# Attention scores from float16 pairs, decay added on GpSimd: one change to a fused attention and feed-forward kernel

## Chip, cores and metric

The kernel runs on one core of a Trainium2 chip. The metric is device time in microseconds (us) of one execution; lower is better. The engines are TensorE (PE; its weight loads are PEld), VectorE (DVE), ScalarE (ACT), GpSimd (POOL) and SyncE (SP), whose queue issues all of this kernel's DMAs in order.

## What is computed

Causal attention with a multiplicative forget gate, then a two-layer feed-forward block, all in float32. There are 8 batches, 8 heads, 576 tokens and 64 columns per head; the feed-forward block goes from 512 to 2048 and back for the 4608 tokens.

```python
scores = scale * np.matmul(q, k.transpose(0, 1, 3, 2))      # scale = 1/8
cum = np.cumsum(np.log(np.clip(f, 0.0001, 1.0)), axis=-1)
decay = cum[:, :, :, None] - cum[:, :, None, :]
scores = np.where(causal, -1000000000.0, scores + decay)
scores = scores - np.max(scores, axis=-1, keepdims=True)
attn = np.exp(scores)
attn = attn / (np.sum(attn, axis=-1, keepdims=True) + 1e-09)
x = np.matmul(attn, v)                                      # heads side by side: 4608 x 512
h = x @ w_in
g = np.where(h >= 1, h, np.where(h <= -1, 0.0, (h + 1) ** 2 / 4))
out = g @ w_out
```

## The kernel before, in words

**Jobs.** The attention is cut into 36 jobs, each a pair of heads of one batch. The first batch is cut in two by rows, so jobs 0 to 3 do its rows 0 to 255 and jobs 4 to 7 the others; from job 8 on each job is a whole pair, four to a batch: batch 1 is jobs 8 to 11, batch 2 jobs 12 to 15. A job goes through blocks of 128 rows (`r` from 0 to 4; the last has 64 rows of both heads stacked on 128 partitions).

**One job.** `load` (L328) brings q and k in two loads and a remainder each, two jobs ahead. `prepare` (L364) turns them with ten TensorE transposes per pair (L374), through PSUM and two ACT copies (L375), into `qkT`: 64 partitions per head, head 0 on partitions 0 to 63 and head 1 on 64 to 127, in float32. `scores` (L409) makes a block's scores by two products into the same PSUM: the float32 product of q and k over 64 rows (L426, `s<-qkT`), and a bfloat16 product over 6 rows (`s<-dec`), whose operands hold 8 times the cumulative log gate in three bfloat16 parts and ones, so that it adds the decay. Those operands are made once by `decay_sums` (L143), written to HBM as `dec_d`, and loaded per job by `load_decay` (L354).

`weights` (L489) takes a block on: a DVE operation (L510) reads the scores from PSUM, adds the causal mask `hide`, scales, keeps the row maximum and writes an SBUF buffer `sdr` (four of them; `sd4`, two, for the last block); ACT does the exponential (L514) and, with the reciprocal sum, the upper float16 half of the weights `pr` (L528), DVE the lower half (L534). A transposing DMA turns them into `pT` (L540, L543), of which there is one buffer, so it waits for the values product of the job before. `values` (L547) is that product (L554): three float16 products, upper by upper, upper by lower and lower by upper, in place of one in float32. Its scale comes from `value_scale` (L255), which loads all of a batch's v through the three buffers `vm` and takes the maximum on DVE (L264). The feed-forward products work on such float16 pairs as well.

**Feed-forward work.** It is done in units of 256 tokens by 256 hidden columns: `moe_front` (L581; 48 or 96 matmuls L596, then ACT, ACT, DVE, ACT, DVE at L605 to L610) and `moe_back` (L617; 12 matmuls L624). Units of finished tokens are spread between the attention blocks; those left over follow the last job.

**Order.** The program is written job by job; a compile-time scheduler then orders each engine's instructions and gives out buffers. An engine runs its list in order. The early jobs, up to about 250 us, run while the weights are loaded and split (`weight_step`), partly on POOL (L242, L243).

Of the kernel before, what the change touches and what calls it, by code (L numbers as in the profile page):

```python
# [16 lines left out]
P = 128  # L17
# [12 lines left out]
NPE = 5  # L30

# [15 lines left out]
def kernel(  # L47
# [93 lines left out]
    dec_d = dram.tile([B * H, NR, 2, S], BF16, name="dec_d")  # L141

    def decay_sums():  # L143
# [5 lines left out]
        rows = rows[0:nb, 0:NR * 2 * S].rearrange("p (r j s) -> p r j s", r=NR, j=2)  # L149
# [11 lines left out]
        rest = fl[0:nb, 0:S]  # L161
        nc.vector.tensor_scalar(out=rest, in0=cum, scalar1=8.0, scalar2=None, op0=ALU.mult)
# [6 lines left out]
        nc.sync.dma_start(dec_d, rows)  # L169


    hide = const.tile([P, FULL], F32, name="hide")
    hide4 = const.tile([P, S], F32, name="hide4")
# [81 lines left out]
    def value_scale(b):  # L255
        m4 = tiny.tile([P, NPAIR], F32, name="m4", bufs=2)
        for i in range(NPAIR):
            if b:
                st = two.tile([P, S], F32, name="vm", bufs=3)
            else:  # L260
                st = stage[:, i * S:(i + 1) * S]
# [11 lines left out]
        scale_of(sv[:, b:b + 1], pv[:, b:b + 1], m)  # L273

# [53 lines left out]
    def load(ji):  # L328
# [3 lines left out]
        w.sps = {}  # L332
# [5 lines left out]
        for j, src in enumerate((q, k)):  # L338
# [5 lines left out]
            dst = x.rearrange("p (t h d) -> p h t d", t=nt, h=2)  # L344
            full = min(w.r1, LAST)
# [8 lines left out]
    def load_decay(w):  # L354
        bh = w.b * H + 2 * w.hp
        w.dec = two.tile([P, 2, S], BF16, name="dec", bufs=3)
        for h in range(2):
            nc.sync.dma_start(w.dec[64 * h:64 * h + NR], dec_d[bh + h])
# [5 lines left out]
    def prepare(w):  # L364

        t_ = two.tile([P, 2, S], F32, name="qkT")
        w.q, w.k = t_[:, 0], t_[:, 1]
# [41 lines left out]
    def scores(w, r):  # L409
# [4 lines left out]
        if r < LAST:  # L414
            outs = [sp[:, h] for h in range(2)]
            w.sps[r] = [sp[:, h, 0:wid] for h in range(2)]
        else:
            flat = sp.rearrange("p h c -> p (h c)")
            outs = [flat[64 * h:64 * h + 64] for h in range(2)]
            w.sps[r] = [flat[:, 0:wid]]  # L420
        for c0 in range(0, wid, 512):
            c1 = min(wid, c0 + 512)
            for x, y, n in ((w.q[:, s0:s1], w.k, D), (w.dec[:, 0, s0 + w.s0:s1 + w.s0], w.dec[:, 1], NR)):
                for h in range(2):
                    rows = slice(64 * h, 64 * h + n)
                    nc.tensor.matmul(  # L426
                        outs[h][:, c0:c1], lhsT=x[rows], rhs=y[rows, c0:c1], start=(n == D), stop=(n == NR)
                    )

# [59 lines left out]
    def weights(w, r):  # L489
# [5 lines left out]
        sds = []  # L495
        for sp in w.sps[r]:
            if r < LAST:
                ring = sdr + more if w.p < NPE else sdr
            else:
                ring = sd4 + [prs[LAST]] if w.p < NPE else sd4  # L500
# [278 lines left out]
```

## Time and profile before

| | |
|---|---|
| median of 3 runs | 1242.38 us (1242.05 to 1242.46) |
| profiled execution: time | 1243.96 us |
| profiled execution: span of the core | 1242.1 us |
| mean granted TensorE clock | 0.959 |
| PE busy | 1151.3 us, 93% of the span |
| DVE busy | 736.0 us, 59% |
| ACT busy | 763.9 us, 62% |
| POOL busy | 46.4 us, 4% |
| DMA queue that moves the data | 42.7% of 16 engines' span |

The profile is one execution with every instruction's start and end. A row of a grouped view reads: line, engine, operation, output and inputs by the program's names, shape, count, then busy time, mean ns of one, and the idle time of the engine just before. Matmuls are pipelined, so the duration of one holds the time through the array too; what a run of matmuls costs is read from the start of its first to the start of what follows.

### The profile page before, as it was taken

The page shows a single profiled execution, that of the slowest core. Times are in us where ns is not written, and L with a number is a line of the kernel's source. Part 1 is how long each engine was busy: PE and PEld are TensorE (multiplying, and loading weights), DVE is VectorE, ACT ScalarE, POOL GpSimd, SP SyncE. Part 2 cuts the span into 40 slices and gives each one's busy share as a digit, 9 for nine tenths or more (in the row PEclk, how much of TensorE's full clock was granted, in tenths as well). Part 3 has the DMA queues.
Part 4 walks back from the last instruction along what each step waited for, and adds up shares of the span by engine and source line. Part 5 has one row for each costly group of instructions (what it writes and reads, how often), then busy time and mean ns, then how long its engine had stood idle before and what let it go on. Part 6 is the DMA issues. An engine that isn't in the chain of part 4 may idle for free.

```text
span 1242.1 us, 23800 instructions
## 1 busy us (share of the span) xinstructions
PE 1151.3 (93%) x9124; PEld 713.1 (57%) x9124; DVE 736.0 (59%) x2063; ACT 763.9 (62%) x1565; POOL 46.4 (4%) x56
## 2 busy tenths in 40 slices
PE   1778677799899999999999999999999999999998
PEld 0544334455466666666666665655666566577665
DVE  6869877777755755565555555566556655522222
ACT  3666545686766666666566556666766666643443
POOL 2021332000000000000000000000000000000000
PEclk9969767799899999999999999999999999999999
DMA  8854454555854444545414433444643443220000
GB/s 259 278 135 102 140 149 112 106 113 119 166 102 101 93 100 83 101 83 101 69 43 73 100 66 77 81 88 86 115 87 82 85 90 68 50 48 2 18 17 17
DMA packets 336817, 118.21 MB, mean 95 GB/s; under 512 B 321296, under 2 KB 321296, under 8 KB 336640
## 3 DMA queue, kind: packets, MB, share of 16 engines
q1 hardware_dynamic: 336704, 116.70, 42.7%
q8 instruction: 71, 1.16, 0.4%
q14 instruction: 42, 0.34, 0.1%
HBM read 56.72 MB, written 10.32 MB: 54 GB/s over the span
## 4 chain that ended last, share of the span: by engine, by line
PE 79%; ACT 1%; DVE 1%; SPq 0%; DMA 0%; issue 0%; ACTq 0%
PE ph L596 30%; PE po L624 29%; PE s L426 8%; PE big L554 5%; PE big L426 4%; PE big L374 3%; ACT pr L528 0%; DVE sdr L510 0%; DMA qk<-in_q_dram 0%; PE s L132 0%; SPq L543 0%; ACT vs L397 0%; DVE ot L637 0%; SPq L390 0%; DVE pr L534 0%
## 5 line engine op out<-in xcount | busy, mean ns | idle before, releaser
L596 PE MATMUL ph<-x,place 128*128 128x256 f16 (+3 forms) x4608 | 436.6, 250 | 6.7 <-ACT x L563 2.9
L624 PE MATMUL po<-place,g 128*128 128x512 f16 x1728 | 411.3, 380 | 3.8 <-ACT g L609 3.7
L596 PEld LDWEIGHTS <-place 128*128 128x128 f16 x4608 | 356.5, 99 | 71.5 <-issue 9.8
L624 PEld LDWEIGHTS <-g 128*128 128x128 f16 x1728 | 163.0, 98 | 172.7 <-issue 6.6
L514 ACT ACTIVATE sdr<-sdr,nm 128x384 f32<-128x384 f32 (+1 forms) x248 | 137.5, 556 | 106.9 <-DVE nm L510 105.3
L607 DVE SCALAR_TENSOR_TENSOR u<-ph,z,u 128x512 f32<-128x512 f32 x136 | 101.8, 749 | 148.1 <-ACT u L606 147.0
L605 ACT ACTIVATE u<-ph,z 128x512 f32<-128x512 f32 x136 | 104.7, 770 | 106.3 <-PE ph L596 105.8
L534 DVE SCALAR_TENSOR_TENSOR pr<-sdr,rc,pr 128x384 f16<-128x384 f32 (+2 forms) x232 | 120.6, 554 | 60.2 <-ACT pr L528 60.2
L609 ACT ACTIVATE g<-u,z 128x512 f16<-128x512 f32 x136 | 97.9, 720 | 93.8 <-DVE u L607 93.8
L610 DVE SCALAR_TENSOR_TENSOR g<-u,z,g 128x512 f16<-128x512 f32 x136 | 102.0, 750 | 78.8 <-ACT g L609 78.7
L528 ACT ACTIVATE pr<-sdr,rc 128x384 f16<-128x384 f32 (+1 forms) x236 | 120.5, 557 | 23.4 <-ACT sdr L514 16.8
L426 PE MATMUL s<-qkT 64*128 64x128 f32 (+3 forms) x512 | 115.9, 504 | 15.0 <-DVE nm L510 11.1
L510 DVE CUSTOM_DVE_ANT_0 sdr<-s,hide 128x384 f32<-128x384 f32 (+1 forms) x248 | 112.3, 490 | 27.0 <-PE s L426 26.9
L606 ACT ACTIVATE u<-u 128x512 f32<-128x512 f32 x144 | 89.8, 624 | 2.6
L374 PE MATMUL big<-ident,qk 128*128 128x128 f32 (+1 forms) x328 | 62.9, 302 | 19.5 <-DMA qk<-in_q_dram 4.5
L522 DVE TENSOR_SCALAR rc<-sm 128x2 f32<-128x2 f32 (+1 forms) x149 | 24.5, 165 | 93.9 <-ACT sdr L514 86.4
L426 PEld LDWEIGHTS <-dec 6*128 6x128 bf16 (+1 forms) x384 | 19.3, 95 | 103.1 <-issue 80.2
L554 PE MATMUL big<-pT,vs 128*64 128x320 f16 (+3 forms) x1098 | 73.3, 284 | 0.5 <-DVE nm L510 0.4
L374 PEld LDWEIGHTS big<-ident,qk 128*128 128x128 f32 (+1 forms) x328 | 42.9, 153 | 45.6 <-issue 23.2
L426 PEld LDWEIGHTS s<-qkT 64*128 64x128 f32 x512 | 44.4, 197 | 42.4 <-DVE nm L510 14.6
L554 PEld LDWEIGHTS <-vs 128*64 128x64 f16 x1098 | 50.2, 112 | 27.9 <-issue 9.7
L375 ACT ACTIVATE qkT<-big 128x576 f32<-128x576 f32 (+2 forms) x72 | 43.4, 603 | 26.1 <-PE big L374 25.8
(142 smaller groups left out, 857.8 us busy)
## 6 DMA issues: line engine op xcount, KB each, us to landing
out_dram<-ot SPq DMA_DIRECT2D x36, 256.0 KB
qk<-in_k_dram SPq DMA_DIRECT2D x64, 128.0 KB
vm<-in_v_dram SPq DMA_DIRECT2D x28, 288.0 KB
v<-in_v_dram SPq DMA_DIRECT2D x62, 128.0 KB
qk<-in_q_dram SPq DMA_DIRECT2D x56, 128.0 KB
place<-in_moe_w_in_dram SPq DMA_DIRECT2D x12, 512.0 KB
place<-in_moe_w_out_dram SPq DMA_DIRECT2D x10, 512.0 KB
x<-in_moe_w_out_dram SPq DMA_DIRECT2D x6, 512.0 KB
```

The source lines that it names most:

```text
L374: nc.tensor.transpose(pt[:, c0:c0 + m], w.x32[j][0:m, c0:c0 + P], ident[0:m, 0:m])
L426: nc.tensor.matmul(outs[h][:, c0:c1], lhsT=x[rows], rhs=y[rows, c0:c1], start=(n == D), stop=(n == NR))
L510: nc.vector.tensor_tensor_reduce(out=a, in0=sp, in1=hide[:, FULL - wid:FULL] if r < LAST else hide4, scale=-0.125, scalar=BIG, op0=ALU.add ...
L514: nc.scalar.activation(a, a, AF.Exp, bias=nm[:, i:i + 1], scale=-1.0, accum_out=sm[:, i:i + 1])
L528: nc.scalar.activation(pr[:, :, 0, i, :], a, AF.Copy, scale=rc[:, i:i + 1])
L534: nc.vector.scalar_tensor_tensor(out=pr[:, :, 1, i, :], in0=a, scalar=rc[:, i:i + 1], in1=pr[:, :, 0, i, :], op0=ALU.mult, op1=ALU.subtract,)
L554: nc.tensor.matmul(av[64 * h:64 * h + 64, at + s0:at + s1], lhsT=w.vs[:, vl, h, t, :], rhs=w.pT[:, t, pl, h, s0:s1], start=(t == 0 and pi ...
L596: nc.tensor.matmul(ph[:, fi, a0:a1], lhsT=wi[fb][:, wl, t, fi * P:(fi + 1) * P], rhs=xs[b][:, t, xl, s0:s0 + a1 - a0], start=(fi == 0 and ...
L605: nc.scalar.activation(u, h, AF.Relu, scale=z.u[:, i:i + 1], bias=z.h[:, i:i + 1])
L607: nc.vector.scalar_tensor_tensor(out=u, in0=h, scalar=z.t[:, i:i + 1], in1=u, op0=ALU.max, op1=ALU.min)
L610: nc.vector.scalar_tensor_tensor(out=g[:, 1], in0=u, scalar=z.r[:, i:i + 1], in1=g[:, 0], op0=ALU.mult, op1=ALU.subtract)
L624: nc.tensor.matmul(po[ch][i], lhsT=g[:, gl, fi * TC + i * P:fi * TC + (i + 1) * P], rhs=wo[fb][:, wl, fi, :], start=(first and fi == 0 and ...
```

## The change

It has three parts.

1. **Decay on POOL from job 8 on.** The cumulative log gates go to HBM in float32 (`cum_d`), and `load_decay` loads one row per head, broadcast to 128 partitions, into a ring of three buffers `ck`. Per block and head, POOL writes the decay of that block into the `sdr` or `sd4` buffer with a `tensor_scalar` (row gate minus column gate, times a scale) and masks the diagonal square with `affine_select`. DVE's operation then takes that buffer where it took `hide`. The 6-row product is left to jobs 0 to 7, and `dec_d` holds 8 heads in place of 64. The column values come from five more TensorE transposes at the start.
2. **q and k in float16 pairs from job 12 on.** `query_scale` loads all of a batch's q and k once more, eight loads through the `ck` ring, with one DVE maximum each, and makes scales by batch. `prepare` then makes the upper halves on ACT and the lower ones on DVE, in one buffer `qs`, and turns them with one transposing DMA into `qkT`. The scores are three float16 products over 64 rows.
3. **Buffers.** `value_scale` uses the `ck` ring, too; the mask `hide` lies in `qs` for the early jobs.

```diff
+NQK = 12
+NDEC = 8
...
     def load_decay(w, h):
+        bh = w.b * H + 2 * w.hp + h
+        if w.p >= NDEC:
+            ck = two.tile([P, S], F32, name="ck", bufs=3)
+            nc.sync.dma_start(ck, cum_d[bh:bh + 1].broadcast_to([P, S]))
...
+    def query_scale(b):
+        ms = tiny.tile([P, 2, NPAIR], F32, name="m8", bufs=2)
+        for j, src in enumerate((q, k)):
+            for i in range(NPAIR):
+                st = two.tile([P, S], F32, name="ck", bufs=3)
...
+                nc.sync.dma_start(st, part)
+                nc.vector.tensor_reduce(
+                    out=ms[:, j, i:i + 1], in_=st, axis=AX.X, op=ALU.max, apply_absolute_value=True
+                )
...
     def prepare(w):
+        t_ = two.tile([P, 2, 2, SP], F16, name="qkT")
+        if w.p >= NQK:
...
+            w.qk = [(t_[:, 0, lq], t_[:, 1, lk]) for lq, lk in ((0, 0), (0, 1), (1, 0))]
+            qs = one.tile([P, 2, 2, SP], F16, name="qs")
+            for j in range(2):
+                sc = sqk[:, j, w.b:w.b + 1]
+                nc.scalar.activation(qs[:, j, 0], w.x32[j], AF.Copy, scale=sc)
+                nc.vector.scalar_tensor_tensor(
+                    out=qs[:, j, 1], in0=w.x32[j], scalar=sc, in1=qs[:, j, 0], op0=ALU.mult, op1=ALU.subtract
+                )
+            nc.sync.dma_start_transpose(
...
     def scores(w, r):
+        terms = [(x[:, s0:s1], y, D) for x, y in w.qk]
+        if w.p < NDEC:
+            terms.append((w.dec[:, 0, s0 + w.s0:s1 + w.s0], w.dec[:, 1], NR))
...
+        for h in range(2):
+            p0, p1 = (0, P) if r < LAST else (64 * h, 64 * h + 64)
+            sd = sds[h % len(sds)][0]
+            nc.gpsimd.tensor_scalar(
+                out=sd[p0:p1, 0:wid], in0=w.ck[h][p0:p1, 0:wid], scalar1=w.nsig if w.p < NQK else w.nsig[p0:p1],
+                scalar2=w.cqs[p0:p1, r, h:h + 1], op0=ALU.mult, op1=ALU.add,
+            )
+            nc.gpsimd.affine_select(
...
```

The order of instructions shows it at two places. The first is PE at a job's first block: `s` is the scores' PSUM, `qkT` the turned q and k, `ph` and `place` a feed-forward product. Before:

```order
L374 MATMUL big<-ident,qk_1_127 128x64
L426 MATMUL s<-qkT 128x128 x2
L426 LDWEIGHTS dec
L426 MATMUL s<-dec 128x128
L426 LDWEIGHTS dec
L426 MATMUL s<-dec 128x128
```

And with the change:

```order
L511 LDWEIGHTS qkT
L511 MATMUL s<-qkT 128x128
L511 LDWEIGHTS qkT
L511 MATMUL s<-qkT 128x128
L511 LDWEIGHTS qkT
L511 MATMUL s<-qkT 128x128
L511 LDWEIGHTS qkT
L511 MATMUL s<-qkT 128x128
L690 LDWEIGHTS place_107
L690 MATMUL ph<-x,place_107 128x256
```

The transposes are gone from PE there, and the float32 product and the 6-row product of two heads have become three float16 products of two heads (the first two of the six lie ahead of these rows), most of them with nothing in between.

The second place is SP, in the later part of the program. Before, between the transposing transfers of two jobs, stand the loads of v, of the next q and k, and of the decay:

```order
L543 DMA_TRANSPOSE pT<-pr_5646 128x10x64 x2
L390 DMA v_128<-in_v_dram 128x4x64 x2
L392 DMA v_128<-in_v_dram 64x2x64
L347 DMA qk_0_126<-in_q_dram 128x4x64 x2
L351 DMA qk_0_126<-in_q_dram 64x2x64
L347 DMA qk_0_126<-in_k_dram 128x4x64 x2
L351 DMA qk_0_126<-in_k_dram 64x2x64
L644 DMA out_dram<-ot 128x512 x2
L358 DMA dec<-dec_d 6x1152 x2
L540 DMA_TRANSPOSE pT<-pr_5761 128x4x128
```

With the change, where `query_scale` falls, in the second job of each batch (`ck` is the ring of three, `cum_d` the gates):

```order
L306 DMA ck<-in_q_dram 128x576
L400 DMA qk_1_133<-in_k_dram 128x4x64
L404 DMA qk_1_133<-in_k_dram 64x2x64
L306 DMA ck<-in_q_dram 128x576
L306 DMA ck<-in_k_dram 128x576 x4
L411 DMA ck<-cum_d 128x576 x2
L436 DMA_TRANSPOSE qkT<-qs 128x20x128
L634 DMA_TRANSPOSE pT<-pr_5342 128x4x128
L634 DMA_TRANSPOSE pT<-pr_5372 128x8x128
```

The loads of the ring, and the transfer that turns q and k, have moved in ahead of the transposing transfers of the weights. DVE's list has the matching eight maxima there, between feed-forward operations.

123 lines of the change are left out of this document (90 added, 33 removed).

## The prediction, as it was put on record

> **What bounds the kernel now.** I read the page first for the busiest engine, then a table by stage, then the stage that is longest. The page gives TensorE:
>
> ```profile
> PE 1151.3 (93%) x9124; PEld 713.1 (57%) x9124; DVE 736.0 (59%) x2063; ACT 763.9 (62%) x1565; POOL 46.4 (4%) x56
> ```
>
> A share of 93% is a mean, so I cut the span in four. The columns are the stretch, its length, then busy time and count of PE, PEld, DVE, ACT and POOL, granted clock, DMA share and GB/s; the last row counts the values product alone.
>
> ```profile
> 0.00:250.00 250.00, 167.72 (x905) 97.69 (x906) 192.35 (x601) 139.12 (x310) 46.44 (x56) 0.82 0.58 160
> 250.00:340.00 90.00, 85.75 (x645) 48.72 (x643) 64.36 (x206) 66.42 (x150) 0.00 (x0) 0.94 0.65 132
> 340.00:1086.00 746.00, 745.98 (x6337) 462.92 (x6333) 435.71 (x1200) 493.14 (x1013) 0.00 (x0) 1.00 0.43 84
> 1086.00:1242.00 156.00, 151.86 (x1246) 103.81 (x1245) 43.58 (x58) 65.24 (x94) 0.00 (x0) 1.00 0.08 22
> ```
> ```profile
> 340.00:1086.00 746.00, 53.24 (x828) 35.81 (x828) 1.00 0.43 84
> ```
>
> From 340 to 1086 us PE has no idle time at full clock, and the other engines have room. The values product has 36 matmuls in a job, so its 828 are 23 jobs: a job takes 746 / 23 = 32.4 us, in which DVE works 18.9, ACT 21.4, and the DMA engines 0.43 x 32.4 = 13.9. What leaves PE here leaves the time, until something else is late. Before 250 us PE is one third idle; the last stretch is feed-forward work, which the change leaves alone.
>
> **What the change takes from PE.** One job on PE in order of time (start, length, then the group; I read from start to start):
>
> ```profile
> 604.99 2.25 PE L554 MATMUL big<-pT,vs 128*64 128x64 f16 x36
> 607.17 2.85 PE L596 MATMUL ph<-x,place 128*128 128x192 f16 x48
> 609.86 2.75 PE L624 MATMUL po<-place,g 128*128 128x512 f16 x12
> ...
> 617.72 0.80 PE L374 MATMUL big<-ident,qk 128*128 128x128 f32 x5
> 618.26 0.54 PE L426 MATMUL s<-qkT 64*128 64x128 f32 x4
> 618.73 0.23 PE L426 MATMUL s<-dec 6*128 6x128 bf16 x2
> 618.89 1.48 PE L596 MATMUL ph<-x,place 128*128 128x192 f16 x23
> 620.21 0.80 PE L374 MATMUL big<-ident,qk 128*128 128x128 f32 x5
> 620.95 0.43 PE L596 MATMUL ph<-x,place 128*128 128x64 f16 x5
> 621.30 0.70 PE L426 MATMUL s<-qkT 64*128 64x256 f32 x4
> 621.94 0.28 PE L426 MATMUL s<-dec 6*128 6x256 bf16 x2
> 622.15 1.29 PE L596 MATMUL ph<-x,place 128*128 128x192 f16 x20
> ...
> 626.30 0.92 PE L426 MATMUL s<-qkT 64*128 64x384 f32 x4
> 627.14 0.33 PE L426 MATMUL s<-dec 6*128 6x384 bf16 x2
> 627.41 2.52 PE L596 MATMUL ph<-x,place 128*128 128x192 f16 x42
> ...
> 632.45 1.13 PE L426 MATMUL s<-qkT 64*128 64x512 f32 x4
> 633.51 0.39 PE L426 MATMUL s<-dec 6*128 6x512 bf16 x2
> 633.83 2.79 PE L596 MATMUL ph<-x,place 128*128 128x256 f16 x24
> ...
> 639.14 1.08 PE L426 MATMUL big<-qkT 64*64 64x512 f32 x4
> 640.15 0.40 PE L426 MATMUL big<-dec 6*64 6x512 bf16 x2
> 640.48 0.33 PE L426 MATMUL big<-qkT 64*64 64x64 f32 x4
> 640.75 0.21 PE L426 MATMUL big<-dec 6*64 6x64 bf16 x2
> 640.89 0.28 PE L596 MATMUL ph<-x,place 128*128 128x256 f16 x1
> ```
>
> The transposes take 0.54 + 0.74 = 1.28 us. The five score blocks take 0.63 + 0.85 + 1.11 + 1.38 + 1.75 = 5.72, of which the decay products are 0.16 + 0.21 + 0.27 + 0.32 + 0.47 = 1.43.
>
> In their place from job 12 on stand three float16 products over 128 + 256 + 384 + 512 + 576 = 1856 columns, both heads side by side. The trace has no such product over 64 rows, so I bound it. The nearest row is L554: float16, two heads side by side, weights of its own for each matmul; it passes 3 x 1600 columns in 2.18 us, 0.454 ns per column with the weight loads in it. So 3 x 1856 columns take 2.53 us. Leaving the 64-row form costs something: the first decay product takes 0.16 for 128 columns worth 0.06, so 0.10 per block; the order has about five groups a job, so 0.5. That makes 3.03, and I take it. The low end is L596, 24 x 256 columns in 2.69, 0.438 ns, with no cost of leaving: 2.44. The high end prices every product like a decay product: 3 x 1.43 = 4.29.
>
> The Trainium skill ("TensorE: Matmul & The Clock Gate", Part 3 on row and column tiling) says that a weight load overlaps matmuls in flight only when it goes to another row group. By it the next product of the same head could not load early, and the price would be near the high end; the L554 row, all 128 rows and the same row groups, disagrees, but it is tiled by columns. It stands below as a rival.
>
> So a job saves 5.72 - 3.03 + 1.28 = 3.97 us, and 24 jobs 95.3. Jobs 8 to 11 lose the decay product alone: 4 x 1.43 = 5.7. Six scales of q and k add two small PE steps each, which I put at 0.5, like the five transposes' 0.54: 3.0. The balance is 98.0; between the ends it is 24 x 2.71 + 5.7 - 3 = 68 and 24 x 4.56 + 5.7 = 115.
>
> **What it adds elsewhere.** The rows for it are groups by shape (busy us, mean ns, idle before), ACT, DVE and POOL in turn:
>
> ```profile
> L375 ACT ACTIVATE qkT<-big 128x576 f32<-128x576 f32 x60 | 38.7, 646 | 22.4 <-PE big L374 22.1
> L397 ACT ACTIVATE vs<-v,sv 128x640 f16<-128x640 f32 x31 | 25.6, 826 | 24.0 <-PE big L554 16.4 <-DVE sv L112 4.3 <-DVE gm L104 2.2
> ```
> ```profile
> L398 DVE SCALAR_TENSOR_TENSOR vs<-v,sv,vs 128x640 f16<-128x640 f32 x31 | 27.3, 882 | 15.6 <-ACT vs L397 15.5
> L264 DVE TENSOR_REDUCE m<-vm 128x1 f32<-128x576 f32 x28 | 20.3, 743 | 10.6 <-DMA vm<-in_v_dram 10.5
> L245 DVE SCALAR_TENSOR_TENSOR place<-place,sw,place 128x512 f16<-128x512 f32 x10 | 7.4, 744 | 1.4 <-ACT place L240 1.4
> L245 DVE SCALAR_TENSOR_TENSOR place<-x,sw,place 128x512 f16<-128x512 f32 x6 | 5.1, 861 | 0.7 <-ACT place L240 0.7
> ```
> ```profile
> L242 POOL TENSOR_SCALAR place<-place,sw 128x512 f32<-128x512 f32 x12 | 9.7, 821 | 106.9 <-ACT place L240 106.9
> ```
>
> With the saving a job would take 32.4 - 4.0 = 28.4 us. ACT trades two copies of 0.646 for two of 0.826: 21.8 us, 77%. DVE gains two lower halves at 0.882, eight maxima per four jobs at 0.743, and as many as four more that the shared ring moves here from the early stage: 18.9 + 1.76 + 1.49 + 0.74 = 22.9, 81%. POOL writes 3712 columns a job at 0.821 / 512 us, which is 6.0, and ten masks that I put at 0.3 (128 columns at that rate are 0.21): 9 us. None is full, so I cost them at nothing while their inputs come in time. If that cover goes, the scores' PSUM is not read, and PE stops at the next score block.
>
> SP's rows (start, time of the issues) for one job before:
>
> ```profile
> 607.27 6.76 SPq L540 DMA_TRANSPOSE pT<-pr  x4
> 614.12 2.96 SPq L543 DMA_TRANSPOSE pT<-pr  x2
> ...
> 639.80 0.94 SPq L644 DMA_DIRECT2D out_dram<-ot  x2
> ```
>
> SP has the weights' transfers out at 617, then issues q, k and v, and is at its next output at 639.80. The new transfer is moved ahead of them: it has 20 squares where those four have 40, so about 3.4 us of issue, for 24 jobs. The transposed weights of that job are used from 644 on, so 3.4 us are hidden by more than 20. On the DMA engines a job adds 0.66 MB of transposing, 0.59 of gates and 0.59 of q and k; at the stage's 84 GB/s for 0.43 of the engines that is 9.4 us, 13.9 to 23.3, or 82%.
>
> The ring is the new wait. While `query_scale` loads, two of its three buffers are free at most, so eight loads go in four rounds, each waiting for a maximum in DVE's list, and behind the loads on SP stand the gates, the turned q and k and the transposed weights. The nearest row is L264: 10.5 us of waiting in 28 maxima, 0.375 each. The 48 new ones then wait 18 us on DVE; I take half of it, 9, as reaching PE, between nothing and the rival below. At the start the smaller `dec_d`, the added gates and five transposes on an idle PE I take at nothing, as also the moved maxima.
>
> The sum: 98 - 9 = 89. The profiled execution took 1243.96, its span 1242.1 and the rest outside; 1243.96 - 89 = 1155, and the median lies 1.6 lower: 1153 us.
>
> **Rivals.** First, exposed weight loads over 64 rows: the high price, 24 x 1.26 = 30 us less gain, 1183. The L554 row speaks against it. Chance 0.12.
>
> Second, loads become late. In the stretch from 250 to 340, with jobs as short as the new ones, PE idled 4.25 us of 90 at a DMA share of 0.65, and the chain of waits has there
>
> ```profile
> 322.18 2.25 DMA qk<-in_q_dram
> ```
>
> That rate, 4.7% of the 648 us that the long stage would have left, is 31 us, for my 9: 1175. If the ring stops PE, a round is 0.6 of issue, 2.25 of load and 0.743 of maximum, four rounds 14.4; half of that in six batches is 43: 1187. Chance 0.20.
>
> Third, it ends slower: POOL holds up DVE. The Trainium skill ("GPSIMD Engine Reference", 1. Specifications) says that the two share their SBUF interfaces, with contention when DVE reads two SBUF inputs, as L534 and L610 do. If DVE stood for all of POOL's 9 us, and 1.5 us a load for three loads a job (four times L264's mean), a job would cost DVE 22.9 + 9 + 4.5 = 36.4, for PE's old 32.4: 24 x 4.0 = 96 slower, 1338. It decides from the point where 5 of POOL's 9 us stop DVE. For it speaks L245, 744 ns in one form and 861 in the other while POOL worked nearby; but 16% of 9 us is 1.4. Chance 0.08.
>
> Fourth, it does not do what it says: the heads' products run one after the other. That doubles 2.53 us: 61 less gain, 1214. The last block's decay product, two heads with 512 columns in 0.33 us where one after the other needs 0.45, speaks against. Chance 0.05.
>
> **How the numbers follow.** The forecast has 0.55: from 1127 (a saving of 115, nothing given back) to some 1170. The range must leave out 2 in 10 at most; from 1128 the first two rivals bring it to 1195, and the other two, 0.13, stay out with the tails. A measurement of this kernel can tell about 0.2% from no change. Faster has the forecast and rivals one, two and four less a little for unclear ends, 0.90; rival three splits into 0.08 slower and, with the rest, 0.02 the same.
>
> **What would show it.** Right: no transposes from job 12 on; score blocks of about 0.27, 0.45, 0.62, 0.80 and 0.88 us from start to start; PE still full from 340 us on, with jobs of about 28 us. Wrong: blocks at three times the decay product; PE idle before score blocks, ended by DVE's L604, with DVE waiting for `ck` loads or POOL; DVE operations with two SBUF inputs longer than now by much more than 16%; or a DMA share near 1.

## The result, and the profile after

| | before | after |
|---|---|---|
| median | 1242.22 us (1241.60 to 1242.46, 4 runs) | 1289.21 us (1283.95 to 1293.72, 4 runs) |
| span of the profiled execution | 1242.1 us | 1285.8 us |
| PE busy | 1151.3 us | 1081.4 us |
| PE idle (span less busy) | 90.8 us | 204.4 us |

The kernel became slower: the ratio is 1.0378, with a 95% interval of 1.0336 to 1.0419. The forecast was 1153 us, 136 less than what came. The last two lines of the table already hold the story: PE works 69.9 us less and idles 113.6 us more, and 113.6 - 69.9 is the 43.7 us by which the span grew. The engines' row of the page after:

```profile
PE 1081.4 (84%) x8859; PEld 688.2 (54%) x8859; DVE 837.0 (65%) x2227; ACT 763.1 (59%) x1564; POOL 373.6 (29%) x620
```

No engine is full any more. So the question goes from "who is busiest" to "what is waited for, and where". The table by stage, with the columns of the prediction's table, and one worse stretch of 50 us below it:

```profile
0.00:250.00 250.00, 172.42 (x932) 101.45 (x933) 187.20 (x585) 139.43 (x310) 68.98 (x102) 0.81 0.55 145
250.00:340.00 90.00, 60.48 (x427) 35.33 (x426) 54.92 (x144) 46.75 (x100) 27.12 (x50) 0.82 0.71 148
340.00:1086.00 746.00, 653.21 (x5861) 420.20 (x5861) 525.04 (x1379) 481.71 (x1003) 270.80 (x455) 0.94 0.70 144
...
300.00:350.00 50.00, 18.07 (x113) 9.73 (x114) 30.56 (x101) 21.69 (x52) 20.43 (x37) 0.58 0.92 187
```

and the same 50 us of the kernel before:

```profile
300.00:350.00 50.00, 45.73 (x400) 27.50 (x398) 37.15 (x125) 36.38 (x81) 0.00 (x0) 0.90 0.66 142
```

In the first 250 us little changed (932 matmuls for 905). From 250 us on PE stands: 29.5 us of 90 (4.3 before), then 92.8 of 746 (none before). The granted clock goes with it, 0.94 in place of 1.00 in the long stage, and 0.58 where PE idles most. There the matmuls themselves are slower, too: the four float32 ones over 512 columns in the first row below take 2.08 us, where the same four took 1.13 in the prediction's rows. The Trainium skill ("TensorE: Matmul & The Clock Gate", Part 1) says that the clock is held down by default and released by a busy PE; these rows agree.

The worst stretch shows one turn of the mechanism. PE first (start, length, group, and in brackets the idle time before and who ended it):

```profile
313.81 2.08 PE L511 MATMUL s<-qkT 64*128 64x512 f32 x4 [3.15 <-DVE nm L604]
323.66 4.26 PE L648 MATMUL big<-pT,vs 128*64 128x64 f16 x36 [7.78 <-DVE nm L604]
328.67 0.39 PE L690 MATMUL ph<-x,place 128*128 128x192 f16 x4 [0.74 <-ACT x L657]
330.71 0.93 PE L511 MATMUL big<-qkT 64*64 64x512 f16 x12 [1.66 <-DVE x L658]
331.57 1.03 PE L690 MATMUL ph<-x,place 128*128 128x192 f16 x8
337.96 0.37 PE L125 MATMUL s<-ident,m 128*1 128x128 f32 x1 [5.36 <-DVE m L287]
```

DVE at the same time:

```profile
315.75 1.15 DVE L628 SCALAR_TENSOR_TENSOR pr<-sdr,rc,pr 128x384 f16<-128x384 f32 x2 [0.73 <-ACT pr L622]
320.96 0.75 DVE L283 TENSOR_REDUCE m<-ck 128x1 f32<-128x576 f32 x1 [4.07 <-DMA ck<-in_v_dram]
321.63 0.68 DVE L604 CUSTOM_DVE_ANT_0 sdr<-s,sdr 128x512 f32<-128x512 f32 x1
...
322.85 0.75 DVE L604 CUSTOM_DVE_ANT_0 sd<-big,sd 128x576 f32<-128x576 f32 x1
...
336.96 0.75 DVE L283 TENSOR_REDUCE m<-ck 128x1 f32<-128x576 f32 x1 [5.09 <-DMA ck<-in_v_dram]
```

And SP's queue:

```profile
305.70 6.59 SPq L634 DMA_TRANSPOSE pT<-pr  x4
312.39 3.15 SPq L637 DMA_TRANSPOSE pT<-pr  x2
315.65 0.53 SPq L411 DMA_DIRECT2D ck<-cum_d  x1
316.28 0.38 SPq L282 DMA_DIRECT2D ck<-in_v_dram  x1
...
324.09 0.52 SPq L282 DMA_DIRECT2D ck<-in_v_dram  x1
...
328.19 0.34 SPq L282 DMA_DIRECT2D ck<-in_v_dram  x1
328.64 4.54 SPq L634 DMA_TRANSPOSE pT<-pr  x3
333.29 0.96 SPq L282 DMA_DIRECT2D ck<-in_v_dram  x1
```

POOL reads the gates in `ck`; the row with `nsig` is of job 12, the one with `cq` of job 11:

```profile
305.81 0.82 POOL L521 TENSOR_SCALAR sd<-ck,nsig,cqs 64x576 f32<-64x576 f32 x1
...
312.62 1.53 POOL L521 TENSOR_SCALAR sdr<-ck,cq 128x512 f32<-128x512 f32 x2
```

At 316 the scores of 512 columns lie ready in PSUM, and the DVE operation that takes them (L604) has its decay written. But ahead of it in DVE's list stands a maximum of v (L283), whose load was issued at 316.28 only, behind six transposing transfers in SP's order. Until 314.15 all three buffers held gates: two those of job 11, which POOL still read, and the third one of job 12, in use since 305.81. DVE stands 4.07 us, then takes the scores of this block and, at 322.85, those of the last one, whose PSUM (`big`) the values product needs; by then PE has idled 7.78. The other three loads of that batch's v follow one by one, at 324, 328 and 333, between other transfers, and the last makes DVE stand 5.09 us and PE 5.36. In the grouped rows this is the idle time before the maxima:

```profile
L307 DVE TENSOR_REDUCE m<-ck 128x1 f32<-128x576 f32 x48 | 36.1, 752 | 42.4 <-DMA ck<-in_q_dram 21.9 <-DMA ck<-in_k_dram 20.5
L283 DVE TENSOR_REDUCE m<-ck 128x1 f32<-128x576 f32 x28 | 21.0, 751 | 32.2 <-DMA ck<-in_v_dram 32.1
```

42.4 + 32.2 = 74.6 us of DVE standing at maxima, where the kernel before had 10.6.

What the change does to PE came as forecast. Score blocks of one or another job, each with the group behind it:

```profile
739.68 0.34 PE L511 MATMUL s<-qkT 64*128 64x128 f16 x6
739.96 0.39 PE L690 MATMUL ph<-x,place 128*128 128x256 f16 x2
...
743.86 0.50 PE L511 MATMUL s<-qkT 64*128 64x256 f16 x6
744.29 1.59 PE L690 MATMUL ph<-x,place 128*128 128x256 f16 x13
...
748.84 0.66 PE L511 MATMUL s<-qkT 64*128 64x384 f16 x6
749.43 2.36 PE L690 MATMUL ph<-x,place 128*128 128x256 f16 x20
...
754.75 0.82 PE L511 MATMUL s<-qkT 64*128 64x512 f16 x6
755.50 2.36 PE L690 MATMUL ph<-x,place 128*128 128x256 f16 x20
...
789.14 0.93 PE L511 MATMUL big<-qkT 64*64 64x512 f16 x12
790.00 0.28 PE L690 MATMUL ph<-x,place 128*128 128x256 f16 x1
```

From start to start 0.28, 0.43, 0.59, 0.75 and 0.86 us, in sum 2.91, for a forecast of 0.27, 0.45, 0.62, 0.80 and 0.88.

### The profile page after: what moved, and what is told of

The parts are those of the page before. It is cut to its first block, busy times and chain, and to the rows that moved or that the text cites. A ratio compares the mean times of both kernels' runs of the same rounds, so it can differ in the third digit from the quotient of the medians.

```text
span 1285.8 us, 24565 instructions
## 1 busy us (share of the span) xinstructions
PE 1081.4 (84%) x8859; PEld 688.2 (54%) x8859; DVE 837.0 (65%) x2227; ACT 763.1 (59%) x1564; POOL 373.6 (29%) x620
## 3 DMA queue, kind: packets, MB, share of 16 engines
q8 instruction: 69, 1.13, 0.4%
## 5 line engine op out<-in xcount | busy, mean ns | idle before, releaser
L690 PE MATMUL ph<-x,place 128*128 128x256 f16 (+3 forms) x4608 | 450.8, 253 | 44.0 <-ACT x L657 25.6
L690 PEld LDWEIGHTS <-place 128*128 128x128 f16 x4608 | 368.8, 101 | 133.2 <-issue 59.7
L521 POOL TENSOR_SCALAR sdr<-ck,nsig,cqs 128x128 f32<-128x128 f32 (+1 forms) x192 | 160.7, 841 | 270.9 <-DVE pr L628 264.6
L628 DVE SCALAR_TENSOR_TENSOR pr<-sdr,rc,pr 128x384 f16<-128x384 f32 (+2 forms) x232 | 125.5, 574 | 34.5 <-ACT pr L622 34.2
L511 PE MATMUL s<-qkT 64*128 64x128 f16 (+5 forms) x704 | 92.3, 363 | 45.1 <-DVE nm L604 40.0
L604 DVE CUSTOM_DVE_ANT_0 sdr<-s,sdr,nalpha 128x128 f32<-128x128 f32 (+1 forms) x192 | 99.6, 546 | 34.3 <-POOL sdr L525 17.3
L521 POOL TENSOR_SCALAR sd<-ck,nsig,cqs 64x576 f32<-64x576 f32 x48 | 44.4, 926 | 233.4 <-DMA ck<-cum_d 162.6
L525 POOL TENSOR_SCALAR_AFFINE_SELECT sdr<-sdr 128x128 f32<-128x128 f32 x224 | 78.1, 360 | 8.4
L511 PEld LDWEIGHTS <-qkT 64*128 64x128 f16 (+1 forms) x864 | 34.7, 100 | 72.8 <-issue 54.3
L307 DVE TENSOR_REDUCE m<-ck 128x1 f32<-128x576 f32 x48 | 36.1, 752 | 42.4 <-DMA ck<-in_q_dram 21.9
L433 DVE SCALAR_TENSOR_TENSOR qs<-qk,sqk,qs 128x640 f16<-128x640 f32 x48 | 42.0, 906 | 17.6 <-ACT qs L432 17.6
```

Source lines behind the costliest of these rows:

```text
L511: nc.tensor.matmul(outs[h][:, c0:c1], lhsT=x[rows], rhs=y[rows, c0:c1], start=(i == 0), stop=(i == len(terms) - 1),)
L521: nc.gpsimd.tensor_scalar(out=sd[p0:p1, 0:wid], in0=w.ck[h][p0:p1, 0:wid], scalar1=w.nsig if w.p < NQK else w.nsig[p0:p1], scalar2=w.cqs[p ...
L604: nc.vector.tensor_tensor_reduce(out=a, in0=sp, in1=other, scale=w.nalpha, scalar=BIG, op0=ALU.add, op1=ALU.min, accum_out=nm[:, i:i + 1],)
L628: nc.vector.scalar_tensor_tensor(out=pr[:, :, 1, i, :], in0=a, scalar=rc[:, i:i + 1], in1=pr[:, :, 0, i, :], op0=ALU.mult, op1=ALU.subtract,)
L690: nc.tensor.matmul(ph[:, fi, a0:a1], lhsT=wi[fb][:, wl, t, fi * P:(fi + 1) * P], rhs=xs[b][:, t, xl, s0:s0 + a1 - a0], start=(fi == 0 and ...
```

## The experiments

Theory 1: the `ck` ring, shared by the gates and the maxima of q, k and v, makes the maxima's loads late, and DVE stands at them. Theory 2: POOL and DVE hold each other up where both access SBUF. Theory 3: the way through the four score buffers has become longer, since POOL must write one before DVE can use it. All runs at a glance; "DVE at maxima" is DVE's idle time before the maxima of q, k and v, summed (L283 and L307 after the change):

| run | median us | 95% interval of the ratio to before | DVE at maxima, us |
|---|---|---|---|
| before | 1242.2 | | 10.6 |
| after | 1289.2 | 1.0336 to 1.0419 | 74.6 |
| two rings of two (rings22) | 1208.5 | 0.9704 to 0.9735 | 21.5 |
| fixed scale (fixed_scale) | 1211.7 | 0.9713 to 0.9765 | 42.3 |
| decay alone (decay_alone) | 1227.0 | 0.9834 to 0.9902 | 30.7 |
| POOL twice (pool_twice) | 1348.9 | 1.0823 to 1.0867 | 73.3 |
| ring of four, shared (ck4) | 1245.3 | 1.0003 to 1.0033 | 64.9 |
| loads spread (spread) | 1270.6 | 1.0180 to 1.0258 | 77.5 |
| two rings, fixed scale (rings22_fixed) | 1179.7 | 0.9462 to 0.9509 | 11.8 |
| pairs alone (pairs_alone) | 1247.4 | 1.0029 to 1.0056 | 33.2 |
| gates from POOL's queue (gates_poolq) | 1290.4 | 1.0334 to 1.0434 | 60.8 |
| two rings, POOL twice (rings22_pool2) | 1221.7 | 0.9791 to 0.9833 | 30.8 |
| two rings, loads held (rings22_hold) | 1221.2 | 0.9795 to 0.9863 | 45.9 |
| the same, gates from POOL's queue (rings22_hold_poolq) | 1235.0 | 0.9914 to 0.9944 | 49.6 |
| three and one (rings31) | 1240.5 | 0.9974 to 1.0004 | 66.4 |
| three and one, fixed scale (rings31_fixed) | 1182.5 | 0.9481 to 0.9551 | 25.1 |
| three and two (rings32) | 1221.3 | 0.9816 to 0.9864 | 33.4 |
| two and three (rings23) | 1207.3 | 0.9693 to 0.9742 | 21.5 |
| a scale by pair (pair_scale) | 1232.0 | 0.9898 to 0.9946 | 82.8 |
| two rings, constants for the scale (rings22_loads) | 1211.4 | 0.9742 to 0.9790 | 34.4 |

The last column alone doesn't give the time: with the loads spread DVE stands 3 us longer than after the change and the kernel is 19 us faster; with the gates from POOL's queue it stands 14 us less and nothing is gained. What stands behind a maximum in DVE's list counts as well.

### Is it the ring, the maxima, or POOL?

**Two rings of two.**

```diff
 def value_scale(b), def query_scale(b):
-                st = two.tile([P, S], F32, name="ck", bufs=3)
+                st = two.tile([P, S], F32, name="vm", bufs=2)
 def load_decay(w, h):
-            ck = two.tile([P, S], F32, name="ck", bufs=3)
+            ck = two.tile([P, S], F32, name="ck", bufs=2)
```

> Two buffers for the gates and two of their own for the maxima of q, k and v, in place of three shared. Theory 1 (the shared ring: the two gates hold two of three buffers until POOL's last write of a job, the maxima's loads go through the third one at a time, and SP, in order, keeps the turned q and k and the turned weights behind them; DVE stands at the maxima): the loads no longer wait for gates, so most of the 122 us of idle TensorE between 250 and 1120 us goes: 1180 to 1230 us. Theory 2 (POOL and DVE hold each other up) and theory 3 (the longer way through the four score buffers, which POOL must write before DVE and gets back only from DVE's lower half): the same as changed, 1275 to 1295.

1208.5 us: 81 us come back, and the kernel is 2.8% faster than the one before. The same loads, the same maxima, the same work on POOL. DVE's rows for the maxima:

```profile
L307 DVE TENSOR_REDUCE m<-vm 128x1 f32<-128x576 f32 x48 | 35.5, 746 | 11.7 <-DMA vm<-in_k_dram 8.0 <-DMA vm<-in_q_dram 3.5
L283 DVE TENSOR_REDUCE m<-vm 128x1 f32<-128x576 f32 x28 | 20.6, 746 | 9.8 <-DMA vm<-in_v_dram 9.8
```

They stand 53 us less, and the time fell by more than that. DVE's operation L604 also waits less for POOL's mask, 6.7 us for 22.4, and at a higher clock (0.931 for 0.915 in the mean) the same 8859 matmuls keep PE busy for 1067.7 us in place of 1081.4. The loads of q and k, issued between 244 and 935 us in the changed kernel, are all issued by 406 us here. It isn't the amount of DMA traffic: in the long stage its share is 0.68 for 0.70, and yet PE idles 31 us there in place of 93:

```profile
340.00:1086.00 746.00, 714.76 (x6571) 455.86 (x6572) 526.54 (x1399) 523.20 (x1081) 275.40 (x469) 0.97 0.68 132
```

Theory 1 holds for the larger part.

**A fixed scale** in place of `query_scale`'s loads, maxima and small steps.

```diff
 def query_scale(b):
-        for j, src in enumerate((q, k)):
...
-        across(mk, m2)
-        sc = sqk[:, :, b]
-        scale_of(sc, mk, mk)
...
+        nc.vector.memset(sqk[:, :, b], 256.0)
+        nc.vector.memset(nsig[:, b:b + 1], -8.0 * 65536.0)
+        nc.vector.memset(nalpha[:, b:b + 1], -0.125 / 65536.0)
```

> q and k are scaled by 256 in every batch: the 48 loads of q and k for the maxima, their 48 maxima and the two small TensorE steps a batch are left out; the maxima of v stay in the shared ring. Theory 1: two thirds of what goes through the ring beside the gates is gone, and with it most of the idle TensorE: 1170 to 1220 us. Theories 2 and 3: POOL's work and the score buffers are as they were; only 48 x 0.74 = 36 us of DVE's 837 go, which is not full: 1265 to 1290.

1211.7 us: 78 us, as theory 1 has it. What is left in the shared ring, the maxima of v, still makes DVE stand 42.3 us.

**The decay alone**, with q and k in float32 to the end.

```diff
-NQK = 12
+NQK = 36
```

> The decay on POOL from batch 1 on, q and k in float32 with transposes on TensorE to the end, as before the change. It leaves out the pairs: no maxima of q and k, no turned q and k by transfer. TensorE loses 28 decay products of 1.43 us, 40 us. Theory 1: the maxima of v still meet the gates in the ring, seven times, which gives back some 10 to 25 us: 1210 to 1235. Theory 2 or 3: POOL's 28 jobs cost what they cost in the changed kernel, and the time is above the one before: 1250 to 1290.

1227.0 us: theory 1's range. POOL and the gates by themselves gain 15 us on the kernel before, though PE works 38 us less (1113.2 for 1151.3).

**POOL's writes twice.**

```diff
+            for _ in range(2):
                 nc.gpsimd.tensor_scalar(
...
                 )
```

> Each of POOL's writes of the decay is made twice, with the same result: POOL works 6 us more a job, 28 jobs. Theory 1: POOL is in use 29% of the time, the second write is late only where DVE waits for POOL now (22 us of DVE's waits in all): 1290 to 1320. Theory 2 (the port): the cost of POOL's work beside DVE doubles: if it is what makes the 140 us between forecast and result, 1370 or more. Theory 3 (the way through the score buffers): 1.6 us more for each 512-column write in a chain of five a job, 3 to 5 us a job: 1370 to 1430.

1348.9 us, 60 more than the changed kernel: above what theory 1 said and below the others. So POOL's time did count, and the next question was by which way. The same two lines of doubling on top of the two rings:

> Two rings of two (1208.5) with each of POOL's writes made twice. In the shared ring that cost 1349 - 1289 = 60 us. If POOL's time is paid by itself, through the score buffers or the port: again 50 to 60, 1260 to 1270. If it is paid through the ring, since the gates' buffers are held until POOL's last write of a job and the maxima wait for them: at most a third of it, 1210 to 1230.

1221.7 us, 13 more than two rings alone, where the shared ring paid 60. So POOL's work is paid mostly through the ring. Not by longer standing at the maxima, though: that is 73.3 us with the doubled writes and 74.6 without. What grew is DVE's wait for POOL's mask, from 22.4 to 58.9 us in the shared ring, and from 6.7 to 14.5 in two rings. A likely reason is that its gates come late in the shared ring: with the doubled writes POOL waits 158 us for them there, and 87 in two rings.

**The pairs alone**, decay on TensorE to the end, maxima in a ring of two.

```diff
-NDEC = 8
+NDEC = 36
...
-    NDH = NDEC // (2 * NPAIR) * H
+    NDH = B * H
...
+    hide = const.tile([P, FULL], BF16, name="hide")
+    hide4 = const.tile([P, S], BF16, name="hide4")
...
-                st = two.tile([P, S], F32, name="ck", bufs=3)
+                st = two.tile([P, S], F32, name="vm", bufs=2)
```

> The pairs as in the changed kernel with the maxima in a ring of two of their own, the decay on TensorE in every batch, so no gates and no POOL; its decay rows are not scaled, so that part of what is computed is left out, and the mask is a constant in bfloat16 in place of float32. It gives back 28 decay products of 1.43 us, 40 us, beside the run with two rings (1208.5): 1248 if POOL and gates cost nothing there; with 55 us lost to POOL's way through the score buffers and to the gates, 1190 to 1200; between these in proportion.

1247.4 us, the 1248 of the case in which POOL and gates cost nothing once the rings are apart. In sum, that is: in the first 250 us PE idles 9 us more than with two rings (99.5 for 90.1), and from there on 12 less (38.0 for 50.1). So theories 2 and 3 can have a share of some 12 us once the rings are apart, as the 13 us for the doubled writes also suggest, but not the bulk.

### What in the ring: the order on SP, the number of buffers, or the eight in a row?

**A ring of four, shared**, at all three places:

```diff
-                st = two.tile([P, S], F32, name="ck", bufs=3)
+                st = two.tile([P, S], F32, name="ck", bufs=4)
```

> One ring of four buffers for gates and maxima, where two rings of two gave 1208.5. If it is the number of buffers that counts: 1200 to 1220. If it is that the maxima stand in the same queue for buffers as the gates, which are held until POOL's last write of a job: the ring gains one buffer for four rounds of loads, two at a time now, and some half of the 80 us come back: 1235 to 1265.

1245.3 us, 44 of the 81: the case in which sharing counts, not only the number. DVE still stands 64.9 us.

**Loads spread**: `query_scale` made a generator that yields behind each maximum, one taken per step.

```diff
             nc.sync.dma_start(st, part)
             nc.vector.tensor_reduce(
                 out=ms[:, j, i:i + 1], in_=st, axis=AX.X, op=ALU.max, apply_absolute_value=True
             )
+            yield
...
+                    scans.append(query_scale(w.b + 1))
+                for _ in range(1 if scans else 0):
+                    if next(scans[0], 0) == 0:
+                        scans.pop()
```

> The ring of three as in the changed kernel, the same loads and maxima, but the eight loads of q and k are written one to a step over two jobs (nine steps) in place of eight at once in one step. Theory 1: a load waits alone for the third buffer and SP and DVE don't stand for eight in a row; the part that q and k have in the loss (78 us by the run with a fixed scale) goes but for the loads themselves: 1210 to 1240. If it is the total of work and loads, or POOL's way through the score buffers, nothing changes: 1275 to 1295.

1270.6 us, a miss: 19 us in place of 50 to 80. It isn't that eight loads stand in a row. One by one they wait as long, 77.5 us in all.

**Gates from POOL's queue.**

```diff
-            nc.sync.dma_start(ck, cum_d[bh:bh + 1].broadcast_to([P, S]))
+            nc.gpsimd.dma_start(ck, cum_d[bh:bh + 1].broadcast_to([P, S]))
```

> The shared ring of three as in the changed kernel, but the gates' loads are issued from POOL's queue in place of SP's. If what costs is that SP stands before a gate's load until a buffer is free, with the turned q, k and weights behind it: 1210 to 1240. If it is the ring itself (the loads for the maxima wait for buffers whose gates are in use, and DVE's list stands at the maxima, whoever issues): 1270 to 1300. POOL then also issues 56 loads, at no price that a run has shown yet.

1290.4 us, no change. I had also held SP's order to be guilty, since the gates stand in it ahead of the turned q, k and weights. Taking them out of it gives nothing in sum: after 250 us PE idles 19 us less (108.1 for 126.8), and in the first 250 us 12 more (90.1 for 77.6). So a part of the loss, up to these 19 us, may lie in SP's order; the rest is not in it.

**On which side of the parted ring a buffer counts.** Three for the gates and one for the maxima:

```diff
-                st = two.tile([P, S], F32, name="ck", bufs=3)
+                st = two.tile([P, S], F32, name="vm", bufs=1)
...
             ck = two.tile([P, S], F32, name="ck", bufs=3)
```

> Three buffers for the gates, one for the maxima (four in all, as with two and two, 1208.5). If the gates hold things up (POOL waited 130 us for their loads with two buffers): 1185 to 1200. If the maxima do, with one buffer each load waits for the maximum before it: 1220 to 1245.

1240.5 us, with four buffers as in two and two. Its rows for the maxima:

```profile
L307 DVE TENSOR_REDUCE m<-vm 128x1 f32<-128x576 f32 x48 | 36.0, 749 | 46.4 <-DMA vm<-in_q_dram 23.4 <-DMA vm<-in_k_dram 22.8
L283 DVE TENSOR_REDUCE m<-vm 128x1 f32<-128x576 f32 x28 | 20.9, 747 | 20.0 <-DMA vm<-in_v_dram 20.0
```

With one buffer, each load starts only when the maximum before it is done, and DVE stands nearly as in the shared ring of four (66.4 for 64.9). So it is the maxima that want the buffers, not the gates. In the shared ring of three the gates of the running job hold two buffers, and the maxima live on the third, when the next job's first gate doesn't hold it. Three and two, and two and three, with the room from the decay rows of the first batch:

```diff
-            w.dec = two.tile([P, 2, S], BF16, name="dec")
+            w.dec = two.tile([P, 2, S], BF16, name="dec", bufs=1)
```

> Three buffers for the gates and two for the maxima; the room comes from the decay rows of batch 0, which have one buffer in place of two (up to 2 us in each of 7 early jobs). If a third gate buffer is worth something beside two for the maxima: 1185 to 1200. If not: 1205 to 1220.

> Two buffers for the gates and three for the maxima, the room from the decay rows as with three and two. If it is the maxima's loads that want buffers: 1190 to 1200, under three and two. If the loads of the maxima are already early enough with two: 1205 to 1220.

1221.3 and 1207.3 us. With a third buffer for the gates the kernel gains nothing; that it loses 13 us I can't explain. Eight of them lie in the first 250 us (PE idles 98.2 us there, for 90.1), where the decay rows have lost a buffer, too; DVE stands 33.4 us at the maxima, for 21.5. With a third one for the maxima it gains 1.2 us, inside the spread of the runs.

### What is left, and where

**Two rings and a fixed scale**, the two edits above together.

> Two rings of two, and a fixed scale of 256: no loads and maxima of q and k at all. If the wait for buffers was their whole cost, it is as with two rings alone: 1200 to 1210. If the rest of the way from 1208 to the forecast 1153 lies in these 48 loads and maxima (36 us on DVE, 14 MB): 1165 to 1185. Theory 3 (the way through POOL and the score buffers) has the rest elsewhere: 1200 to 1210.

1179.7 us: the 48 loads and maxima cost another 29 even with a ring of their own. Is that due to where they stand? In the run with two rings the scheduler had drawn 32 of these loads into the first 250 us (24 by 200 us, not the 32 that the expectation below has there). Its first stage, by the columns of the table by stage:

```profile
0.00:250.00 250.00, 159.86 (x807) 89.93 (x809) 198.54 (x598) 124.74 (x278) 55.72 (x81) 0.79 0.67 182
```

So the first two loads of each batch were held back, by a copy of one column of the running job's k into their buffers:

```diff
-    def query_scale(b):
+    def query_scale(b, after):
...
                 st = two.tile([P, S], F32, name="vm", bufs=2)
+                if j == 0 and i < 2:
+                    nc.vector.tensor_copy(st[:, 0:1], after[:, 0:1])
```

> Two rings of two, and the first two loads of q and k of each batch held back by a copy of one column from the k of the running job into their buffers, so that they can't be issued in the first 200 us, where the run with two rings had three batches of them (32 loads) and was 26 us later than the changed kernel at job 9. If those early loads are what made that start late: 1180 to 1195, near the run with a fixed scale (1179.7). If the loads cost the same wherever they stand: 1205 to 1215.

The same stage and the long one of that run:

```profile
0.00:250.00 250.00, 165.63 (x872) 95.59 (x873) 188.58 (x595) 134.75 (x302) 65.47 (x96) 0.80 0.58 152
...
340.00:1086.00 746.00, 700.71 (x6383) 441.55 (x6380) 532.87 (x1394) 508.69 (x1047) 266.43 (x452) 0.99 0.72 144
```

1221.2 us, a miss. The start did get better, as expected: its DMA share falls from 0.67 to 0.58, PE does 65 matmuls more, and the last score block of job 12 came at 319.7 us in place of 344.2. But from there on the kernel took 36 us more (1219.4 - 319.7 against 1207.9 - 344.2), PE idling 45 of 746 us. Loads that ran ahead in the start were the cheaper ones. The run also bounds what that lead is worth: the loads go on until 849 us here, and that costs 13 us beside two rings alone, the copies included. The other 68 of the 81 us come back without it. With the gates from POOL's queue on top:

> The held loads and two rings of two, with the gates issued from POOL's queue: SP loses 56 issues of some 0.5 us. If SP's order still holds something back once the rings are apart, 5 to 20 us less than with SP's queue alone; if not, the same within 5 us; more, if POOL's issue of loads stands before its writes.

1235.0 us, 14 more: SP's order holds nothing back here either, and loads issued from POOL cost something. PE's idle time grows by 13 us, 9 of them in the first 250 us (93.6 for 84.4). By which way I did not separate.

**A scale for each pair**, from the q and k in SBUF (two maxima of 128x640 a job, 24 scales, no loads):

```diff
+        for j in range(2):
+            nc.vector.tensor_reduce(
+                out=m2[:, j:j + 1], in_=w.x32[j], axis=AX.X, op=ALU.max, apply_absolute_value=True
+            )
+        mk = tiny.tile([P, 2], F32, name="mk", bufs=2)
+        across(mk, m2)
```

> Two rings of two, and a scale for each job (24) in place of each batch (6), from the q and k that the job has loaded anyway: two maxima of 128x640 a job and four times as many small steps, no loads for it. If the 29 us between 1208.5 and 1179.7 are the 48 loads: 1180 to 1195. If they are the scale's own work (maxima on DVE, small steps that TensorE waits for in its order): 1210 to 1240.

1232.0 us: without the loads it is slower still. But not by the small steps: the maxima now wait for the job's own q and k, and DVE stands longer than in any other run.

```profile
L304 DVE TENSOR_REDUCE m2q<-qk 128x1 f32<-128x640 f32 x48 | 39.2, 817 | 71.2 <-DMA qk<-in_q_dram 58.6 <-DMA qk<-in_k_dram 10.4 <-issue 1.9
```

With the 11.6 us at the maxima of v that makes 82.8. So this run doesn't weigh the loads against the scale's steps; it shows once more what a maximum costs whose load has no lead. To see the small steps by themselves, they alone were left out of the kernel with two rings:

```diff
-        across(mk, m2)
-        sc = sqk[:, :, b]
-        scale_of(sc, mk, mk)
...
+        nc.vector.memset(sqk[:, :, b], 256.0)
```

> Two rings of two, with the 48 loads and maxima of q and k as they are, but the scale itself is a constant 256: the two small steps on TensorE and the ten on DVE that make a scale of the maxima are left out, and nothing waits for the maxima's result. With the steps it took 1208.5, without loads and maxima too 1179.7. If the loads and maxima are what costs: 1200 to 1210. If it is the small steps and the wait for the scale: 1178 to 1190.

1211.4 us, just above the first range, and 3 us more than with the steps. So six scales' small steps cost nothing that can be seen, and the 29 us lie in the loads and maxima. Between load and maximum they are not parted.

**Three and one, fixed scale**, again two edits above together.

> Three buffers for the gates, one for the maxima of v, a fixed scale of 256 for q and k, so their 48 loads and maxima are left out. With two and two that took 1179.7. If the last 27 us to the forecast lie in gates that come late: 1155 to 1170. If they lie in the start and in the jobs with little feed-forward work, where the way through one job is longer than its TensorE work: 1175 to 1185.

1182.5 us: the last 27 us to the forecast don't lie in late gates, as far as this run tells; with one buffer the maxima of v stand 25.1 us for 11.8, which may hide a small gain. In the run with two rings and a fixed scale PE idles 118.1 us in all, 27 more than before the change, where the sum had 9; and it works 87 us less, where the sum had 98. Two stretches of that run show where it idles:

```profile
300.00:350.00 50.00, 33.41 (x273) 20.60 (x270) 38.25 (x120) 32.69 (x74) 25.39 (x41) 0.79 0.96 195
340.00:1086.00 746.00, 728.87 (x6772) 466.39 (x6772) 505.78 (x1300) 525.45 (x1070) 261.63 (x457) 0.99 0.65 125
```

PE idles 16.6 us of the 50 where the kernel before idled 4.3, and 17.1 of the 746 where it idled none: 29 us more, some of it counted in both stretches. In the first, PE had 273 matmuls for 400 before, at a DMA share of 0.96 for 0.66. Whether it is the transfers there or the lack of feed-forward work to fill in stays open.

## Why the prediction was wrong

**What was right.** PE's saving: 2.91 us of scores a job for the 3.03 taken, and no transposes from job 12 on. With the ring out of the way PE's busy time shows it: 1151.3 - 1064.5 = 87 us with two rings and a fixed scale, at a clock still below 1 in the start. So weight loads over 64 rows are hidden for the most part, as the row of L554 said; the Trainium skill's rule on row groups ("TensorE: Matmul & The Clock Gate", Part 3), the first rival, does not hold for these blocks, at 2.91 us where its price was 4.29. The heads' products run side by side; the fourth rival falls with the same rows.

**The step that failed** is the price of the ring, 9 us, where parting the ring brought back 81: "The nearest row is L264: 10.5 us of waiting in 28 maxima, 0.375 each. The 48 new ones then wait 18 us on DVE; I take half of it, 9, as reaching PE". Three things in it were off.

First, the row. L264's loads had a ring of their own, and 23 of those 28 were issued in the first 250 us, long before use. Their 0.375 us is the wait of loads that run ahead. In the shared ring only 4 of the 28 were issued by then, the last at 1010 us, and the 48 new maxima waited 42.4 us, 0.88 each. Two things go into that: with two rings and the lead they wait 0.24, with two rings and the loads held back 0.61. So the lead and the sharing each cost something, and the row showed neither.

Second, the 28 maxima of v were moved into the same ring and taken "at nothing, as also the moved maxima". The prediction counted that they move out of the early stage, but only with their busy time. They wait 32.2 us for the 10.6 of before. Together DVE stands 64 us more, not 18.

Third, the half. DVE's list is in order, and the operation that empties the scores' PSUM stands behind the maximum. The half is not borne out: 64 us more of DVE standing came with 113.6 us more of PE's. How the rest arises is in part argued. POOL gets its score buffers back later, so gates are held longer and the next load is later still; rings22_pool2 against pool_twice (13 us against 60) fits such a loop, which no run took apart. The clock falls, too: 14 us of PE's busy time, by the same matmuls with two rings.

**The sum, as the runs split it.** Of the 136 us between 1153 and 1289, 81 go with the parted ring (rings22), 29 more with the 48 loads and maxima (rings22_fixed), and 27 stay open: idle time of PE for the larger part, and a saving of 87 us of work where 98 were forecast. Only the first was in the sum, as 9; the work of the new loads and maxima was put at nothing.

**The rivals.** The second, "if the ring stops PE", was the right mechanism, at 43 us with a chance of 0.20. Its working counted q and k alone and again halved; v's loads and the loop through POOL were not in it. Its 1187 lies on the faster side, so the range ended at 1195, on the wrong side of the kernel before. The third had the right sign by the wrong cause. The waits after the change have L604 on POOL's mask (L525) for 22.4 us in all, less than 1 us a job, and pairs_alone leaves some 12 us to POOL's work and the gates once the ring is parted.

**"None is full, so I cost them at nothing while their inputs come in time"** was the sentence to distrust. DVE at 65% and POOL at 29% were never full. In the worst stretch a single late load in DVE's list stopped PE at once. That PE had too little other work ready there is my reading; no run tests it.

## What to carry to other kernels

A ring of buffers is also an order: what shares it waits for its neighbours, and can no longer run ahead of them. Before loads are moved into another ring, look at how far ahead they run now, and at how long the neighbours hold a buffer; the wait that they show today is the price with that lead and without those neighbours. And a wait in the middle of an engine's list is priced by what stands behind it: here two rings of two, one buffer more, turned 3.8% slower into 2.8% faster, where the same buffer in one shared ring only made up for the loss.

## What the runs showed of the hardware

One price of DVE came out clean and a second one in its rough size, because jobs with and without POOL, and with a constant or a column of factors, stand in one kernel. After the change:

```profile
L604 DVE CUSTOM_DVE_ANT_0 sdr<-s,sdr,nalpha 128x512 f32<-128x512 f32 x48 | 34.1, 745 | 0.7 <-PE s L511 0.7
L628 DVE SCALAR_TENSOR_TENSOR pr<-sdr,rc,pr 128x256 f16<-128x256 f32 x56 | 28.0, 535 | 11.1 <-ACT pr L622 10.8
L604 DVE CUSTOM_DVE_ANT_0 sdr<-s,sdr 128x512 f32<-128x512 f32 x8 | 5.2, 684 | 0.0
```

With the pairs alone, where POOL does none of it:

```profile
L604 DVE CUSTOM_DVE_ANT_0 sdr<-s,hide,nalpha 128x512 f32<-128x512 f32 x48 | 34.0, 745 | 3.1 <-PE s L511 3.0
L628 DVE SCALAR_TENSOR_TENSOR pr<-sdr,rc,pr 128x256 f16<-128x256 f32 x56 | 24.6, 480 | 9.0 <-ACT pr L622 8.6 <-DMA qk<-in_q_dram 0.5
```

With POOL's writes twice in the shared ring, and with its writes once in two rings:

```profile
L629 DVE SCALAR_TENSOR_TENSOR pr<-sdr,rc,pr 128x256 f16<-128x256 f32 x56 | 30.4, 581 | 9.7 <-ACT pr L623 9.6
```
```profile
L628 DVE SCALAR_TENSOR_TENSOR pr<-sdr,rc,pr 128x256 f16<-128x256 f32 x56 | 24.8, 482 | 8.9 <-ACT pr L622 8.9
```

The 60 ns that L604 became longer look at first like DVE and POOL holding each other up. They aren't: with a constant factor and POOL at work (jobs 8 to 11) it takes 684 ns, as before, and with the column `nalpha` and POOL idle 745. A factor read from SBUF, in place of a constant, costs this operation 60 ns.

L628, which reads two inputs from SBUF, does feel POOL, but little. Over all its widths, 261 operations, it takes 145 us with POOL's writes left out (pairs_alone), 149 to 152 with them once (rings22, the changed kernel), and 157 to 159 with them twice (rings22_pool2, pool_twice). Which width grows differs from run to run: the 256 columns above take 535 ns in the changed kernel, but 482 with two rings, where POOL writes as much. The Trainium skill ("GPSIMD Engine Reference", 1. Specifications) names such instructions as those that contend; the runs agree, at 4 to 14 us of this kernel's time on DVE.
